# Reordering the first batch of a fused attention and MLP kernel

## The chip, the cores and the metric

The kernel runs on one NeuronCore of a Trainium2 chip. The metric is the device time in microseconds (us) of one execution; lower is better. The engines are TensorE (PE, with its weight loads PEld), VectorE (DVE), ScalarE (ACT), GpSimd (POOL) and the queue engine SyncE (SP), which issues most DMAs. Each engine works through its own list of instructions in order; a wait for another engine holds up everything behind it in that list.

## The reference

Eight batches of block-recurrent cross attention are followed by an MLP with a softplus-erf activation. All arithmetic is float32; the two MLP weights arrive as float64 and are turned into float32 in the kernel.

```python
# x: (B=8, H=8, S=512, D=64), state: (8, 8, Ns=32, 64)
scores = x @ state^T / sqrt(D);  a  = softmax over the 32 states
xread  = a @ state                                   # 512 rows per batch and head
scores2 = state @ x^T / sqrt(D); a2 = softmax over the 512 tokens
sread  = a2 @ x                                      # 32 rows per batch and head
tokens = concat([xread, sread], axis=2)              # (8, 8, 544, 64) -> (4352, 512)

h  = tokens @ w_in                                   # w_in (512, 2048)
sp = softplus(h)
out = (h * erf(sp)) @ w_out                          # w_out (2048, 512)
```

The kernel doesn't form xread. For each batch it multiplies the state with w_in first (the "M sets", four per batch, one for each group of 512 hidden features), and the hidden layer of the 512 tokens is then `a @ M`.

## The kernel before

Batch 0 is written out by hand, since the weights have to be fetched and converted at the same time. Sixteen pieces of 1 MB come in the order w_in 0, w_in 1, w_out 0, w_out 1, w_in 2, and so on; in the code they are `"i", 0`, `"o", 0` and so on. A piece passes through one of three raw buffers. It is converted by two ScalarE and three VectorE instructions, and the third VectorE instruction of one piece calls `fetch()` for the next.

```python
def weight(dst, src, shape):
    raw = act.tile([...], U32, name="raw", bufs=3)
    fetched.append(nc.sync.dma_start(out=raw..., in_=src...))
    ...
    return [ACT: dst = hi * 2**-112,  ACT: lo = lo * 2**-29], \
        [DVE: d <<= 3,  DVE: d += lo,  DVE: d |= sign of hi]        # written short here

def on_act(kind, j, ks=range(2)):
    for k in ks: made[kind, j][0][k]()
def on_dve(kind, j, ks=range(3)):
    for k in ks:
        made[kind, j][1][k]()
        if k == 2: fetch()
```

The first batch's attention: x's chunks are turned on TensorE, the scores of all heads are made by 16 small matmuls, and VectorE and ScalarE do the softmax over the states. `between` are pieces of other work, called at fixed places.

```python
for c in range(NC):
    (nc.scalar, nc.sync)[c % 2].dma_start(out=x_t[0][:, c], in_=x[0, :, P * c:P * c + P]...)
    if c == 1:
        for e in range(2):
            nc.sync.dma_start(out=st[:, 0, D * e:D * e + D], in_=state[0]...)

def attention0(between):
    ...
    for c in range(NC):
        for i in range(NI):
            nc.tensor.transpose(out=xp[i][:, P * c:P * c + P], in_=xt[:, c, 2 * i:2 * i + 2, :], identity=ident)
        if c == 1:
            states(range(1))                      # turn and copy state 0
    for i in range(NI):
        (nc.scalar.copy, nc.vector.tensor_copy)[i % 2](xT[:, i, :], xp[i])
    s2 = scored(0, xT)
    between[0]()                                  # 20 warming matmuls; w_in 0 on ACT
    for e in range(2):
        nc.vector.transpose(out=both[:, e], in_=s2[e])
        nc.vector.reduce_max(out=m1, in_=a, axis=AX.X)
        nc.vector.tensor_tensor(a, a, over(m1), op=ALU.subtract)
        nc.scalar.activation(out=a, in_=a, func=ACTF.Exp, scale=scale)
        nc.scalar.copy(sc[:, e], s2[e])
    between[1]()                                  # w_in 1 on ACT, w_in 0 on DVE
    for e in range(2):
        normalise(...)                            # sum, add 1e-9, reciprocal, multiply
        nc.vector.transpose(out=aT[0][:, e], in_=both[:, e])
```

An M set takes 16 matmuls for its two PSUM banks and a copy of each bank. For each of the 16 feature tiles of batch 0, `first0` makes the hidden values of 512 tokens with two matmuls, `soft` and `keep_h` read them from PSUM with ScalarE and VectorE, `erf` and `times` finish the activation, and `project` multiplies with w_out.

```python
def mixed_part(b, g, j, parts, copy):            # part j of M set g
    for i in range(NI):
        for e in range(2):
            nc.tensor.matmul(out=ps[e][q, :], lhsT=st[r, b, q], rhs=w_in[r, fs, i, :], ...)
    return nc.scalar.copy(mg[:, 0], ps[0]), copy(mg[:, 1], ps[1])

# the middle of batch 0, group 1 and the start of group 2 (cut from the whole)
done(project(g0[0], 0, acc, range(NC), range(2)))
on_dve("o", 1); times(Z, g0)
for j in 2, 3:
    convert("i", j)
done(project(g0[0], 0, acc, range(3), range(2, 4)))
on_act("o", 2)
mixed(0, 1, copy=nc.scalar.copy)                 # a whole M set
done(project(g0[0], 0, acc, range(3, 4), range(2, 4)))
...
for i in range(GF):
    first0(2, i, g2[0]); soft(i, g2); keep_h(i, g2); on_dve("o", 5, ...)
```

Up to this point the order of each engine's list is fixed to that of the code (`in_order`). From batch 1 on, `hidden7` and `project7` do 2x2 block products with seven instead of eight multiplications. They need differences of blocks: of M (`combine_m`), of the attention weights (`combine_a`) and, once for all batches, of w_out (`combine_w`):

```python
def combine_w():
    sub(T[1], B12, B11); sub(T[2], B22, T[1]); sub(T[4], B21, T[2])    # 128x2048 each
    def last():
        sub(B12, B22, B12); T[3] = B12
    return last

# after batch 0
in_order(begun)
next(turn)
combine_m(1, 1 - begins(1))
last = behind(at, combine_w)
for b in range(1, B + 1):
    ...  # hidden7 of one group runs while project7 of the one before is stepped
```

Of the kernel before, what the change touches and what calls it, by code (L numbers as in the profile page):

```python
# [16 lines left out]
def kernel(  # L17
# [90 lines left out]
    for c in range(NC):  # L108
        (nc.scalar, nc.sync)[c % 2].dma_start(
            out=x_t[0][:, c], in_=x[0, :, P * c:P * c + P].rearrange("h p d -> p h d"))  # L110
        if c == 1:
            for e in range(2):
                nc.sync.dma_start(out=st[:, 0, D * e:D * e + D],
                                  in_=state[0].rearrange("(i e) n d -> e i n d", e=2)[e])
# [76 lines left out]
    def scored(b, xT):  # L191


        s2 = [ps_at.tile([P, S], F32, name="at") for _ in range(2)]
        for i in range(NI):
            for e in range(2):
                r, q = slice(D * e, D * e + D), slice(Ns * i, Ns * i + Ns)
                on_pe = nc.tensor.matmul(out=s2[e][q, :], lhsT=st[r, b, q], rhs=xT[r, i, :],  # L198
                                         start=True, stop=True)
        marks.append(on_pe)  # L200
        return s2
# [10 lines left out]
    def normalise(a):  # L212
        z1 = small.tile([P, NC * NI], F32, name="z1")
        nc.vector.reduce_sum(out=z1, in_=a, axis=AX.X)
        nc.vector.tensor_scalar(z1, z1, 1e-9, None, op0=ALU.add)
        nc.vector.reciprocal(z1, z1)
        return nc.vector.tensor_tensor(a, a, over(z1), op=ALU.mult)  # L217
# [54 lines left out]
    def attention0(between):  # L272
# [7 lines left out]
        for c in range(NC):  # L280
            for i in range(NI):
                nc.tensor.transpose(out=xp[i][:, P * c:P * c + P],
                                    in_=xt[:, c, 2 * i:2 * i + 2, :], identity=ident)
            if c == 1:
                states(range(1))
        for i in range(NI):
            (nc.scalar.copy, nc.vector.tensor_copy)[i % 2](xT[:, i, :], xp[i])
        s2 = scored(0, xT)
# [3 lines left out]
        aT[0] = keep.tile([P, 2, S], F32, name="aT")  # L292
        for e in range(2):
            nc.vector.transpose(out=both[:, e], in_=s2[e])
            a = both[:, e].rearrange("p (k n) -> p k n", n=Ns)
            m1 = small.tile([P, NC * NI], F32, name="m1")
            nc.vector.reduce_max(out=m1, in_=a, axis=AX.X)
            nc.vector.tensor_tensor(a, a, over(m1), op=ALU.subtract)
            nc.scalar.activation(out=a, in_=a, func=ACTF.Exp, scale=scale)
            nc.scalar.copy(sc[:, e], s2[e])  # L300
        between[1]()
        for e in range(2):
            normalise(both[:, e].rearrange("p (k n) -> p k n", n=Ns))
            nc.vector.transpose(out=aT[0][:, e], in_=both[:, e])
# [22 lines left out]
    def attention(b, xT=None):  # L327
# [10 lines left out]
        aT[b] = keep.tile([P, 2, S], F32, name="aT")  # L338
        for e in range(2):
            nc.vector.transpose(out=both[:, e], in_=sc[:, e])  # L340
            a = both[:, e].rearrange("p (k n) -> p k n", n=Ns)
            m1 = small.tile([P, NC * NI], F32, name="m1")
            nc.vector.reduce_max(out=m1, in_=a, axis=AX.X)  # L343
            nc.vector.tensor_tensor(a, a, over(m1), op=ALU.subtract)  # L344
            nc.scalar.activation(out=a, in_=a, func=ACTF.Exp, scale=scale)
        z2 = weigh_tokens(sc, largest(sc), both[:, 2:4])
        for e in range(2):
            normalise(both[:, e].rearrange("p (k n) -> p k n", n=Ns))
            nc.vector.transpose(out=aT[b][:, e], in_=both[:, e])  # L349
# [18 lines left out]
    def mixed(b, g, parts=1, copy=nc.vector.tensor_copy):  # L368

        m_t[b, g] = mix.tile([P, 2, gw], F32, name="m")  # L370
        return [mixed_part(b, g, j, parts, copy) for j in range(parts)]

    def mixed_part(b, g, j, parts, copy):
# [9 lines left out]
        return nc.scalar.copy(mg[:, 0], ps[0]), copy(mg[:, 1], ps[1])  # L383
# [143 lines left out]
    def combine_w():  # L527
        T[1], T[2], T[4] = (act.tile([P, 2 * GF * P * 2], U32, name="raw", bufs=3).bitcast(F32)
                            .rearrange("p (g i e) -> p g i e", i=GF, e=E2) for _ in range(3))
        sub = lambda o, x, y: nc.vector.tensor_tensor(o, x, y, op=ALU.subtract)  # L530
        sub(T[1], B12, B11)
        sub(T[2], B22, T[1])
        sub(T[4], B21, T[2])

        def last():
            sub(B12, B22, B12)
            T[3] = B12
        return last
# [59 lines left out]
    def begins(b):  # L598
        return 1 - b % 2
# [31 lines left out]
    def prepare(b, g, copy):  # L631
        for j in range(2):
            mixed(b, 2 * g + j, copy=copy)
        combine_m(b, g)

# [59 lines left out]
    def after_scores():  # L695
        warm(20)
        on_act("i", 0)

    def before_sums():
        on_act("i", 1)  # L700
        on_dve("i", 0)

    rest = attention0((after_scores, before_sums))
    m_t[0, 0] = mix.tile([P, 2, gw], F32, name="m")
    mixed_part(0, 0, 0, 2, nc.scalar.copy)
    warm(6)
    on_act("o", 0)
    g0 = group()
    first0(0, 0, g0[0])
    first0(0, 1, g0[0])  # L710
    soft(0, g0)
    on_dve("i", 1)
    on_act("o", 1, [0])
    keep_h(0, g0)
    soft(1, g0)
    mixed_part(0, 0, 1, 2, nc.scalar.copy)
    on_dve("o", 0, [0])
    keep_h(1, g0)
    on_dve("o", 0, [1, 2])
    first0(0, 2, g0[0])  # L720
    first0(0, 3, g0[0])
    erf(A, g0)
    times(A, g0)
    on_act("o", 1, [1])
    for i in 2, 3:
        soft(i, g0)
        keep_h(i, g0)
    erf(Z, g0)
    acc = tiles(NC)
    done(project(g0[0], 0, acc, range(NC), range(2)))  # L730
    on_dve("o", 1)
    times(Z, g0)
    for j in 2, 3:
        convert("i", j)
    done(project(g0[0], 0, acc, range(3), range(2, 4)))
    on_act("o", 2)
    mixed(0, 1, copy=nc.scalar.copy)
    done(project(g0[0], 0, acc, range(3, 4), range(2, 4)))
    on_dve("o", 2)
    on_act("o", 3)  # L740
    g1 = group()
    first0(1, 0, g1[0])
    first0(1, 1, g1[0])
    soft(0, g1)
    keep_h(0, g1)
    on_dve("o", 3, [0, 1])
    soft(1, g1)
    keep_h(1, g1)
    on_dve("o", 3, [2])
    first0(1, 2, g1[0])  # L750
    first0(1, 3, g1[0])
    erf(A, g1)
    times(A, g1)
    on_act("i", 4)
    for i in 2, 3:
        soft(i, g1)
        keep_h(i, g1)
# [3 lines left out]
    convert("i", 5)  # L761
    done(project(g1[0], 1, acc, range(NC), range(2)))
    done(project(g1[0], 1, acc, range(2), range(2, 4)))
    on_act("o", 4)
    mixed(0, 2, copy=nc.scalar.copy)
    done(project(g1[0], 1, acc, range(2, 3), range(2, 4)))
    on_dve("o", 4)
    load_st()
    on_act("o", 5)
    g2 = group()  # L770
    for i in range(GF):
        first0(2, i, g2[0])
        soft(i, g2)
        keep_h(i, g2)
        on_dve("o", 5, range(i, i + 1) if i < 3 else ())
    done(project(g1[0], 1, acc, range(3, 4), range(2, 4)))
    load_xq(1)
# [5 lines left out]

    finish_(g2)
    next(rest)
    done(project(g2[0], 2, acc, range(1)))
    convert("i", 6)
    for bs in range(1, 5), range(5, B):
        states(bs)
    convert("i", 7)  # L790
    done(project(g2[0], 2, acc, range(1, 3)))
    next(rest)
    on_act("o", 6)
    mixed(0, 3, copy=nc.scalar.copy)
    next(rest)
    on_dve("o", 6)
    xT, _ = turn_x(1)
    g3 = group()
    for i in 0, 1:
        first0(3, i, g3[0])  # L800
        soft(i, g3)
        keep_h(i, g3)
    next(rest)
    load_x(1)
    for i in 2, 3:
        first0(3, i, g3[0])
        if i == 2:
            on_act("o", 7)
            on_dve("o", 7, [0, 1])
        soft(i, g3)  # L810
        keep_h(i, g3)
    on_dve("o", 7, [2])
    done(project(g2[0], 2, acc, range(3, 4)))
    finish_(g3)

    turn = attention(1, xT)
    next(turn)
    next(turn)
    seconds = project(g3[0], 3, acc)
# [4 lines left out]

    some(4)
    for k in range(2):
        for j in range(2):
            mixed(1, 2 * (begins(1) ^ k) + j, copy=nc.scalar.copy)
            some(2 if not k else 1)
        if k == 0:  # L830
            combine_m(1, begins(1))
            at = [combine_a(1)]
    in_order(begun)
    next(turn)
    combine_m(1, 1 - begins(1))
    last = behind(at, combine_w)
# [5 lines left out]
    for b in range(1, B + 1):  # L842
# [4 lines left out]
        for g, (first, second) in enumerate(groups):  # L847
# [3 lines left out]
            if b + 1 < B:  # L851

                if g == 0:
                    turn = attention(b + 1)
                    side[6 - (b == 1)] = lambda: behind(marks, next, turn)
                elif g == 1:
                    side[0] = lambda: (next(turn), next(turn))
# [14 lines left out]
            gT_ = first(lambda: next(steps))  # L872
            done(steps)
            if last is not None:
                last()
                last = None
# [34 lines left out]
```

## Time and profile before

The time is 759.62 us, the median of 3 runs (758.96 to 761.93); the profiled execution spans 758.7 us.

| what | value |
|---|---|
| matmul of one projection step (128x512) | about 0.86 us of stream, two records |
| seven-product matmuls, 128x256, 480 of one kind | 118.1 us busy, mean 380 ns |
| conversion of one piece on ACT | 2 instructions, 1.15 us each |
| conversion of one piece on DVE | 0.69, 1.23 and 1.23 us |
| difference of w_out blocks, 128x2048 | 2.29 us |
| load of one weight piece, issue to landing | 4.7 to 5.6 us (median by kind) |
| HBM read and written | 33.03 MB and 8.91 MB |

In the profile each row of a timeline has the start, the length, the engine, the line of the kernel, the operation, what it writes and reads, and in brackets how long its engine sat idle before it and what ended that. L672 is `first0`, L679 `keep_h`, L676 `soft`, L685 `times`, L508 `project`, L381 the M sets, L150 the last conversion step, L452 the matmuls of `hidden7`, L460 its additions, L530 the differences of w_out and L558 `project7`. A wait table has the waiting instruction, who released it, the total in us, how often, and the longest. A TensorE float32 matmul can show as two records.

### The profile page before, as it was taken

The page shows a single profiled execution, that of the slowest core. Times are in us where ns is not written, and L with a number is a line of the kernel's source. Part 1 is how long each engine was busy: PE and PEld are TensorE (multiplying, and loading weights), DVE is VectorE, ACT ScalarE, POOL GpSimd, SP SyncE. Part 2 cuts the span into 40 slices and gives each one's busy share as a digit, 9 for nine tenths or more (in the row PEclk, how much of TensorE's full clock was granted, in tenths as well). Part 3 has the DMA queues.
Part 4 walks back from the last instruction along what each step waited for, and adds up shares of the span by engine and source line. Part 5 has one row for each costly group of instructions (what it writes and reads, how often), then busy time and mean ns, then how long its engine had stood idle before and what let it go on. Part 6 is the DMA issues. An engine that isn't in the chain of part 4 may idle for free.

```text
span 758.7 us, 11976 instructions
## 1 busy us (share of the span) xinstructions
PE 733.8 (97%) x4934; PEld 585.1 (77%) x4934; DVE 524.7 (69%) x775; ACT 390.4 (51%) x488; POOL 0.7 (0%) x6
## 2 busy tenths in 40 slices
PE   7899899799999999999999999999999999999997
PEld 5333343687888888888888888888888889999996
DVE  3887888786759476876677665866696765585423
ACT  3878784485444634644355545554365444443330
POOL 0000000000000000000000000000000000000000
PEclk9999999899999999999999999999999999999999
DMA  7565752261024100610052003310021000000000
GB/s 225 167 222 183 183 133 40 55 130 32 22 61 82 27 29 2 140 29 29 1 108 57 16 17 72 79 20 29 20 65 29 29 1 29 1 29 1 21 8 28
DMA packets 139165, 46.38 MB, mean 61 GB/s; under 512 B 126696, under 2 KB 130536, under 8 KB 139112
## 3 DMA queue, kind: packets, MB, share of 16 engines
q1 hardware_dynamic: 136744, 44.78, 23.6%
q10 hardware_dynamic: 2368, 0.85, 0.5%
q8 instruction: 38, 0.62, 0.3%
q14 instruction: 15, 0.12, 0.1%
HBM read 33.03 MB, written 8.91 MB: 55 GB/s over the span
## 4 chain that ended last, share of the span: by engine, by line
PE 82%; DVE 6%; ACT 2%; issue 0%; DVEq 0%; ACTq 0%
PE o L558 47%; PE h L452 26%; PE at L381 3%; PE o L508 2%; PE h L672 1%; PE at L257 1%; DVE raw L530 1%; PE at L198 1%; DVE hs L460 0%; DVE aT L349 0%; DVE xT L344 0%; DVE xT L217 0%; DVE xT L340 0%; DVE m L343 0%; DVE m L222 0%
## 5 line engine op out<-in xcount | busy, mean ns | idle before, releaser
L459 ACT ACTIVATE s<-hs 128x512 f32<-128x512 f32 x120 | 75.6, 630 | 105.9 <-DVE hs L460 105.5
L558 PE MATMUL o<-w_out,s 128*128 128x256 f32 x480 | 118.1, 380 | 0.0
L558 PE MATMUL o<-raw,hs 128*128 128x256 f32 x480 | 117.0, 385 | 0.1
L503 DVE TENSOR_TENSOR s<-s,hs 128x2048 f32<-128x2048 f32 x30 | 68.8, 2292 | 68.4 <-ACT s L502 68.4
L558 PE MATMUL o<-w_out,hs 128*128 128x256 f32 x480 | 114.1, 380 | 0.0
L558 PEld LDWEIGHTS o<-raw,hs 128*128 128x128 f32 x480 | 88.8, 190 | 32.3 <-issue 19.3
L558 PEld LDWEIGHTS o<-w_out,hs 128*128 128x128 f32 x480 | 90.6, 190 | 16.4 <-issue 4.2
L452 PEld LDWEIGHTS h<-aT,m 128*128 128x128 f32 x672 | 85.7, 194 | 11.2 <-DVE hs L460 4.6
L460 DVE TENSOR_TENSOR hs<-hs,h 128x512 f32<-128x512 f32 x90 | 61.5, 684 | 46.6 <-PE h L452 46.6
L452 PE MATMUL h<-aT,m 128*128 128x128 f32 x672 | 87.8, 279 | 4.7 <-DVE hs L460 3.8
L558 PEld LDWEIGHTS o<-w_out,s 128*128 128x128 f32 x480 | 84.6, 191 | 8.1
L460 DVE TENSOR_TENSOR hs<-s,h 128x512 f32<-128x512 f32 x60 | 41.1, 685 | 42.0 <-PE h L452 41.4
L508 PE MATMUL o<-w_out,s 128*128 128x512 f32 x128 | 59.1, 602 | 2.5 <-DVE s L685 2.5
L452 PE MATMUL h<-sy,sx 128*128 128x128 f32 x448 | 59.7, 275 | 1.2 <-ACT hs L468 0.7
L452 PEld LDWEIGHTS h<-sy,sx 128*128 128x128 f32 x448 | 56.7, 192 | 3.7 <-ACT hs L468 1.5
L558 PE MATMUL o<-raw,s 128*128 128x256 f32 x240 | 57.6, 379 | 0.0
L502 ACT ACTIVATE s<-s 128x2048 f32<-128x2048 f32 x30 | 57.3, 1911 | 0.3
L468 ACT COPY hs<-h 128x512 f32<-128x512 f32 x30 | 17.6, 587 | 77.0 <-PE h L452 77.0
L463 ACT COPY s<-h 128x512 f32<-128x512 f32 x30 | 17.5, 582 | 76.9 <-PE h L452 76.9
L508 PEld LDWEIGHTS o<-w_out,s 128*128 128x128 f32 x128 | 23.0, 190 | 35.5 <-issue 26.7
L558 PEld LDWEIGHTS o<-raw,s 128*128 128x128 f32 x240 | 43.5, 190 | 4.7
L459 ACT ACT_TABLE_LOAD x32 | 41.1, 1283 | 0.6
(120 smaller groups left out, 904.9 us busy)
## 6 DMA issues: line engine op xcount, KB each, us to landing
raw<-in_moe_w_in_dram SPq DMA_DIRECT2D x8, 1024.0 KB, 5.6
raw<-in_moe_w_out_dram SPq DMA_DIRECT2D x8, 1024.0 KB, 4.7
xq<-in_x_dram SPq DMA_DIRECT2D x112, 64.0 KB, 2.1
x<-in_x_dram SPq DMA_DIRECT2D x56, 128.0 KB, 2.7
out_dram<-ot SPq DMA_DIRECT2D x18, 256.0 KB, 2.1
sc<-xT SPq DMA_DIRECT2D x112, 32.0 KB, 1.9
out_dram<-ot SPq DMA_DIRECT2D x28, 128.0 KB, 1.7
x<-in_x_dram ACTq DMA_DIRECT2D x2, 256.0 KB, 5.2
```

The costliest lines, as they stand in the source:

```text
L198: on_pe = nc.tensor.matmul(out=s2[e][q, :], lhsT=st[r, b, q], rhs=xT[r, i, :], start=True, stop=True)
L257: nc.tensor.matmul(out=sr[q, e, :], lhsT=a2T[:, e, c, q], rhs=xt[:, c, 2 * i + e, :], start=(c == 0), stop=(c == NC - 1))
L381: nc.tensor.matmul(out=ps[e][q, :], lhsT=st[r, b, q], rhs=w_in[r, fs, i, :], start=True, stop=True)
L452: last = nc.tensor.matmul(out=bank[:, q], lhsT=lhsT, rhs=rhs, start=(first and i == 0 and k == 0), stop=(i == GF - 1 and k == len(ops) - 1 ...
L459: nc.scalar.activation(out=s[:, k], in_=hs[:, k], func=ACTF.Softplus)
L460: add = lambda o, x, y: nc.vector.tensor_tensor(o, x, y, op=ALU.add)
L463: nc.scalar.copy(m1, p)
L468: nc.scalar.copy(c11, p)
L502: return (nc.scalar.activation(out=s, in_=s, func=ACTF.Erf), nc.vector.tensor_tensor(s, s, hs, op=ALU.mult))
L503: nc.vector.tensor_tensor(s, s, hs, op=ALU.mult))
L508: nc.tensor.matmul(out=acc[r], lhsT=gT[:, i, P * r:P * r + P], rhs=w_out[:, GF * g + i, :], start=(g == 0 and i == 0), stop=(g == NG - 1 a ...
L558: nc.tensor.matmul(out=acc[bank][:, E2 * c:E2 * c + E2], lhsT=lhs[:, i, :], rhs=rhs[:, g, i, :], start=(first and i == 0 and c == 0), stop ...
```

## The change

It reorders the first batch and the passage into the second, and leaves the sum of the mathematics as it is. Its purposes: to have x complete sooner; to let VectorE and ScalarE alternate in the softmax; to make an M set available by halves, each after one weight piece; to keep VectorE's copies from waiting for ScalarE; and to take the long differences of w_out out of the way of the second batch's additions.

```diff
     for c in range(NC):
         (nc.scalar, nc.sync)[c % 2].dma_start(... x chunk c ...)
-        if c == 1:
-            for e in range(2):
-                nc.sync.dma_start(out=st[:, 0, D * e:D * e + D], ...)
+    for e in range(2):
+        nc.sync.dma_start(out=st[:, 0, D * e:D * e + D], ...)
...
-        for i in range(NI):                      # scored
+        for i in reversed(range(NI)):
...
+    def states_weights(b, sc, both):             # also used by the later batches
+        for e in range(2):
+            nc.vector.transpose(out=both[:, e], in_=sc[e])
+        for e in range(2):
+            nc.vector.reduce_max(out=m1[:, e], in_=a[:, e], axis=AX.X)
+        for e in range(2):
+            nc.vector.tensor_tensor(a[:, e], a[:, e], over(m1[:, e]), op=ALU.subtract)
+            nc.scalar.activation(out=a[:, e], in_=a[:, e], func=ACTF.Exp, scale=scale)
...
+    def normalise(a, between=lambda: None):      # both halves share add and reciprocal
+        for e in range(2):
+            nc.vector.reduce_sum(out=z1[:, e], in_=a[:, e], axis=AX.X)
+        between()
         nc.vector.tensor_scalar(z1, z1, 1e-9, None, op0=ALU.add)
         nc.vector.reciprocal(z1, z1)
+        for e in range(2):
+            nc.vector.tensor_tensor(a[:, e], a[:, e], over(z1[:, e]), op=ALU.mult)
...
-        for c in range(NC):                      # attention0
+        for c in 1, 0, 2, 3:
             ... transposes of chunk c ...
-            if c == 1:
-                states(range(1))
         ... copies of xT ...
+        states(range(1))
...
     def after_scores():
-        warm(20)
+        warm(28)
         on_act("i", 0)
     def before_sums():
         on_act("i", 1)
-        on_dve("i", 0)
+        on_dve("i", 0, [0, 1])
+    def amid_sums():
+        on_dve("i", 0, [2])
+        on_act("o", 0, [0])
+        m_t[0, 0] = mix.tile([P, 2, gw], F32, name="m")
+        mixed_part(0, 0, 0, 2, nc.scalar.copy, nc.scalar.copy)
-    mixed_part(0, 0, 0, 2, nc.scalar.copy)
-    warm(6)
-    on_act("o", 0)
```

In the groups of batch 0 the same calls are set in a new order, with M sets 1 to 3 in halves. `evict(i, gT, True)` calls `keep_h` before `soft`. The core of it:

```diff
-    for j in 2, 3:
-        convert("i", j)
-    done(project(g0[0], 0, acc, range(3), range(2, 4)))
-    on_act("o", 2)
-    mixed(0, 1, copy=nc.scalar.copy)
-    done(project(g0[0], 0, acc, range(3, 4), range(2, 4)))
+    convert("i", 2)
+    on_act("i", 3)
+    on_act("o", 2, [0])
+    some0(0, g0, range(2), range(2, 4))
+    mixed_part(0, 1, 0, 2, nc.scalar.copy, nc.scalar.copy)
+    some0(0, g0, range(2, 3), range(2, 3))
+    on_dve("i", 3)
+    load_st()                                    # states 1 to 7, was in group 2
+    on_act("o", 2, [1])
+    first0(1, 0, g1[0])
+    on_dve("o", 2, [0])
+    evict(0, g1, True)
+    mixed_part(0, 1, 1, 2, nc.scalar.copy, nc.scalar.copy)
...
+    for bs in range(1, 5), range(5, B):
+        states(bs)                               # was after group 2
...
+    load_xq(1)                                   # was after group 2's hidden values
...
-    turn = attention(1, xT)                      # after group 3's activation
-    next(turn)
-    next(turn)
-    seconds = project(g3[0], 3, acc)
-    some(4)
-    ... four M sets of batch 1, with 2, 2, 1, 1 steps after them ...
+    turn = attention(1, xT)                      # ahead of group 3, taken in four steps
+    ...
+    some(2)
+    ... four M sets of batch 1, with 3, 3 and 4 steps between and after ...
```

The differences of w_out and of the second M pair, in the passage to batch 1:

```diff
-    def combine_w():
-        sub(T[1], B12, B11); sub(T[2], B22, T[1]); sub(T[4], B21, T[2])
-        def last(): sub(B12, B22, B12); T[3] = B12
+    def combine_w(g, last=False):                # half g: 128x1024 each
+        if last:
+            sub(T[3], B22, B12)
+        else:
+            sub(T[1], B12, B11); sub(T[2], B22, T[1]); sub(T[4], B21, T[2])
...
-    combine_m(1, 1 - begins(1))
-    last = behind(at, combine_w)
...
             gT_ = first(lambda: next(steps))
+            if b == 1 and g == 0:
+                combine_m(1, 1 - begins(1))
+                behind(marks, combine_w, begins(1))
             done(steps)
+            if b == 1 and g == 0:
+                combine_w(begins(1), True)
+            if b == 1 and g == 1:
+                behind(marks, combine_w, 1 - begins(1))
+                behind(marks, combine_w, 1 - begins(1), True)
```

`marks` are the last matmul and the last addition of the `hidden7` just written; `behind` keeps the differences after them. In the later batches `attention` is taken in five steps instead of three, with the same work but for the shared add and reciprocal, and the second batch's scores move two steps up (`side[6 - (b == 1)]` to `side[6 if b > 1 else 3]`).

## The prediction

> **What bounds the kernel now.** I read the shares of busy time first, then the 40 slices, then a table of stretches, TensorE's waits, and last the timeline where TensorE stood still.
>
> ```profile
> PE 733.8 (97%) x4934; PEld 585.1 (77%) x4934; DVE 524.7 (69%) x775; ACT 390.4 (51%) x488; POOL 0.7 (0%) x6
> ...
> PE   7899899799999999999999999999999999999997
> ```
>
> TensorE is the bound: 25 us of 758.7 are idle, nearly all in the first nine slices of 19 us, which is where the change works. The stretches (length, busy time of each engine, granted clock, DMA share, GB/s) say how much there is to win:
>
> ```profile
> 24.00:34.00 10.00, 8.31 (x35) 3.01 (x33) 9.74 (x12) 8.47 (x11) 0.00 (x0) 1.00 0.39 135
> 34.00:83.00 49.00, 45.56 (x128) 17.89 (x128) 37.23 (x41) 37.78 (x41) 0.00 (x0) 1.00 0.64 203
> 83.00:127.50 44.50, 42.03 (x247) 17.02 (x248) 37.49 (x57) 34.01 (x53) 0.00 (x0) 1.00 0.54 119
> 127.50:154.00 26.50, 20.93 (x184) 16.36 (x183) 22.48 (x25) 11.80 (x16) 0.00 (x0) 0.87 0.31 70
> 154.00:200.00 46.00, 44.44 (x288) 38.62 (x288) 36.27 (x62) 28.14 (x36) 0.00 (x0) 1.00 0.31 64
> 200.00:700.00 500.00, 499.86 (x3609) 428.18 (x3608) 349.19 (x535) 242.56 (x302) 0.00 (x0) 1.00 0.17 38
> ```
>
> Length less PE busy gives the idle time: 1.7, 3.4, 2.5, 5.6 and 1.6 us, then 0.1 us in 500. From 127.5 to 154 the mean clock is 0.87, which costs another 0.13 x 26.5 = 3.4 us. So between 24 and 200 us there are 14.8 + 3.4 = 18.2 us that a perfect order could win; before 24 us everything hangs on the softmax. Who ends TensorE's waits between 24 and 154 us:
>
> ```profile
> PE h L452 <- DVE hs L460: 4.8, 2, 3.8
> PE o L508 <- DVE s L685: 2.5, 4, 1.6
> PE h L672 <- DVE hs L679: 1.6, 3, 0.6
> PE at L381 <- DVE w_in L150: 1.5, 2, 1.1
> ```
>
> The first line is one event, and VectorE's timeline shows its cause:
>
> ```profile
> 129.66 2.29 DVE L530 TENSOR_TENSOR raw<-w_out 128x2048 f32<-128x2048 f32 x1
> ...
> 132.47 2.29 DVE L530 TENSOR_TENSOR raw<-w_out,raw 128x2048 f32<-128x2048 f32 x1
> ...
> 136.47 2.29 DVE L530 TENSOR_TENSOR raw<-w_out,raw 128x2048 f32<-128x2048 f32 x1
> 138.67 0.68 DVE L460 TENSOR_TENSOR hs<-s,h 128x512 f32<-128x512 f32 x1
> 139.27 2.29 DVE L530 TENSOR_TENSOR w_out<-w_out 128x2048 f32<-128x2048 f32 x1
> ```
>
> The four differences of w_out for the seven-product scheme sit in one block of VectorE. The addition that frees a PSUM bank (L460) stands behind them until 138.67, so TensorE waits 3.8 us at 139.41, 1.0 us more at 142.21, and then runs at half clock.
>
> **What the skill says.** The Trainium skill, "TensorE: Matmul & The Clock Gate", Part 1: The HAM clock gate, says that after an idle window of about 3.4 us the array's clock is halved until it has been busy about as long. The trace agrees: the granted clock is 0.50 from 140 to 146 us, after the gap of 3.8 us; it is also 0.50 from 21 to 23 us after a gap of only 2.8 us. The same page's "Architectural detail" has VectorE and ScalarE as strict first-in first-out queues; the L460 line behind the block is that. "ScalarE: Activation LUTs", What ACT_TABLE_LOAD costs, gives 1283 ns for a load and some 1380 ns of drain; the trace shows 32 loads of 1283 ns and no drain on top (a load at 54.88, the erf at 56.17). "DMA: Bandwidth & Descriptors", Issuing engines are not separate DMA queues, says that several issuers save only issue time; here one issue takes 0.46 to 0.74 us.
>
> **The change part by part.**
>
> *Loads and scores.* Before, the two loads of state 0 were issued ahead of x's chunk 3 (1.25 to 2.59 us), so chunk 3 was issued at 2.63. Now it goes out at about 1.25, the state after it, and the state's transpose stands after x's. Before, chunks 2 and 3 were turned from 8.10 to 10.02, behind the state's transpose, which waited 0.6 us for its load. I estimate their end at 9.0. The bytes are the same, so I don't expect more. The score matmuls ran from 10.05 to 12.88 (2.83 us), with VectorE's second copy of xT arriving at 10.9; the same 16 matmuls take 1.09 us later (110.25). With all operands there at 10.0, I put their end at 11.3: 1.6 us earlier.
>
> *Softmax halves alternated.* The six VectorE operations take 4.15 us (13.02 to 17.17) in either order; only ScalarE's exponential is better hidden. Then before: conversion of the first w_in piece (0.69, 1.23, 1.23, net 3.2), and two chains of sum, add, reciprocal, multiply, transpose at 2.6 us each, ending 25.58; 12.6 us in all. After: 4.15 + 3.15 + two sums 1.25 + one add and reciprocal 0.45 + two multiplies 1.25 + two transposes 1.3 = 11.55 us, from 11.3 to 22.85. The second aT is 2.7 us earlier. Against that, 28 warming matmuls at 0.25 us (20 took 5.01) end at 18.3, and the six that followed the first M set are gone: two gaps near 1.5 and 1.5 us with 0.7 us of work between, about the activity at which the clock fell before. I take off 0.7 us. **Net 2.0 us.**
>
> *M sets in halves, both copies on ScalarE, and the new order to 127 us.* A half needs one converted w_in piece instead of two: this aims at the 1.1 us at 47.78 (L381 on L150). VectorE copies come before ScalarE's softplus, so they no longer wait for it (VectorE idles 11.9 us ahead of them in the trace), which aims at the three L672 waits (1.6 us). Projections cut finer and set between other work aim at the four L508 waits (2.5 us). Idle from 24 to 127.5 is 7.6 us. Costs: a half takes 0.67 us against 1.09 for a whole, so 2 x 0.67 - 1.09 = 0.25 us each, 0.75 for three sets; one more table load on ScalarE (exponentials between softplus calls), 1.3 us, off TensorE's path. VectorE and ScalarE are busy 37 of 49 us from 34 to 83, so I expect new waits of about 3 us. 7.6 - 0.75 - 3 = **about 4 us.** As a second way I laid the three queues out row by row in program order with these durations (conversion 2.1 us on ScalarE and 3.1 on VectorE, copy 0.6, softplus 0.5, table 1.28, hidden matmul pair 1.8, projection 0.9), each step starting when its engine and its inputs are free: w_in's second piece ready at 25.9, first product and projection at 31.2 (before 34.2), second M set's first half at 42.0 (47.8), last hidden pair of group 2 done at 73.5 (81.2), group 1's projections done at 78.9 (82.8), and the seven-product stage begun at 120.3 (127.5) with 12 of 16 last projections done instead of 10. That is 9.0 us by then, start included, against 6.0 of my sum; it has no time between an event and the engine it frees, so I take it as the bright end.
>
> *States' loads and reads earlier.* Their DMAs are issued on the same queue as the weights: eight of about 0.6 us (5 us) and sixteen (10.5 us by the row of 16 issues at 126.57). The weights then lie two pieces ahead, so I count nothing.
>
> *Block differences in two parts.* 8.8 us of VectorE become two halves of 4 x 1.15 = 4.6 us, each held behind the seven-product stage's last addition. The idle 5.6 us and the half clock 3.4 us of 127.5 to 154 are 9.0 us. What stays: only 4 projection steps (0.86 us each) are left as filler instead of 6, while additions, softplus, table, erf (1.9) and multiply (2.3) take some 7 us before the first product can use them; the next group's products can fill most of it, as they did at 145.8 to 153.7. And the second 4.6 us fall into a stretch where VectorE was already full (10.0 of 10 us from 150 to 160) with batch 2's softmax. I leave 2.5 us: **about 6.5 us.**
>
> *From 200 us on.* One add and one reciprocal less per batch on VectorE, scores in reversed order: TensorE is 100% busy, so nothing.
>
> Sum: 2.0 + 4.0 + 6.5 = 12.5 us, 759.6 to 747.1; with a little of the bright end, **746.8 us**.
>
> **The rivals.**
> - *The wait moves to VectorE later.* The second part of the differences delays additions in 145 to 175 us, and a new gap, perhaps again with half clock, appears there. For: that stretch's full VectorE. Against: the differences are needed only at the third product of the following stage, and VectorE has 0.3 of its time free from 200 us on. It gives back 4 to 6 us: 751 to 753.
> - *The front of the kernel is worse.* Fewer warming matmuls around the first M set bring half clock into the first softplus matmuls, four of 1.7 us: 2 to 3 us, 749 to 750.
> - *ScalarE becomes the bound to 127 us*, with all copies of the M sets and of the conversions on it, in strict order. For: 9.9 of 10 us from 30 to 40. Against: over 34 to 83 it has 11 us free. The middle then brings 0 to 1: 750.
> - *All fits.* 16 to 17 us: 743.
>
> **Range and chances.** The rivals are not exclusive, and one half of each is likely; the ceiling is 18.2 + 2.7 = 21 us. 741.5 to 752 should hold it 8 times in 10. The line of 2% is 744.4 us, 15.2 us of gain: above my sum, below the layout. Faster by over 2%: 0.32; within: 0.65; slower: 0.03.
>
> **What would show it.** Right: no block of three 2.29 us differences, clock 1.00 through the start of the seven-product stage, first softplus matmul near 22 us, stage start near 120 to 122, idle of 24 to 127.5 at 3 to 4 us. Wrong: first softplus matmul still near 24 us or run at clock 0.5; more than 3 us of waits on L460's successor in 140 to 180; or a PE busy sum from 200 on that differs by over 2 us, which I have not counted at all.

## The result and the profile after

The changed kernel takes 750.2 us (median of 4 runs, 749.22 to 751.17) against 760.09 us for the kernel before in the same comparison: ratio 0.987, 95% interval 0.984 to 0.989. I had predicted 746.8 us with a range of 741.5 to 752. The gain is 9.9 us where my sum had 12.5. The two profiled executions span 758.7 and 749.4 us, 9.3 us apart.

The same stretches as before, from the changed kernel's table of stretches (length, then busy time of PE, PEld, DVE, ACT, POOL, then granted clock, DMA share, GB/s):

```profile
24.00:34.00 10.00, 9.12 (x36) 3.50 (x35) 9.84 (x13) 8.07 (x11) 0.00 (x0) 1.00 0.61 190
34.00:83.00 49.00, 48.19 (x174) 20.23 (x173) 39.15 (x47) 44.29 (x57) 0.00 (x0) 1.00 0.74 218
83.00:127.50 44.50, 43.55 (x287) 19.11 (x287) 38.72 (x58) 30.55 (x47) 0.00 (x0) 1.00 0.46 106
127.50:154.00 26.50, 23.51 (x202) 18.96 (x201) 22.16 (x33) 16.56 (x24) 0.00 (x0) 0.94 0.53 122
154.00:200.00 46.00, 44.17 (x301) 36.45 (x301) 37.21 (x53) 23.26 (x28) 0.00 (x0) 1.00 0.11 24
200.00:700.00 500.00, 499.07 (x3616) 430.62 (x3615) 344.69 (x519) 241.26 (x301) 0.00 (x0) 1.00 0.17 38
```

Length less PE busy: 0.9, 0.8, 0.9, 3.0, 1.8 and 0.9 us, where it was 1.7, 3.4, 2.5, 5.6, 1.6 and 0.1; the clock of the fourth stretch costs 0.06 x 26.5 = 1.6 us instead of 3.4. From 24 to 200 us that is 9.1 us lost instead of 18.2. The first three stretches are nearly clean. What is left lies in the passage to batch 1, and it is another wait than before. TensorE's waits from 24 to 154 us, the longest first:

```profile
PE h L457 <- ACT s L468: 1.9, 1, 1.9
PE h L674 <- DVE aT L313: 1.6, 1, 1.6
PE h L674 <- ACT m L387: 1.1, 2, 0.5
PE at L197 <- DVE sn L279: 1.0, 1, 1.0
PE h L457 <- ACT hs L473: 0.7, 1, 0.7
```

The wait on VectorE's addition is down from 4.8 to 0.4 us, that on `times` from 2.5 to 0.2, and those on the copies of the first batch (1.6) and on the converted w_in (1.5) are gone. In their place TensorE waits for ScalarE to copy a bank (L468). ScalarE's timeline shows why it is late:

```profile
133.64 1.91 ACT L507 ACTIVATE s<-s 128x2048 f32<-128x2048 f32 x1
135.46 0.57 ACT L522 COPY ot<-o 128x512 f32<-128x512 f32 x1
135.92 0.59 ACT L468 COPY s<-h 128x512 f32<-128x512 f32 x1
```

The copy stands behind the first group's erf and one copy of a finished output tile. TensorE's own timeline of that place:

```profile
130.77 1.02 PE L513 MATMUL o<-w_out,s 128*128 128x512 f32 x2
131.63 1.05 PE L457 MATMUL h<-aT,m 128*128 128x128 f32 x8
132.53 1.06 PE L457 MATMUL h<-sy,sx 128*128 128x128 f32 x8
133.51 1.10 PE L273 MATMUL at<-x,sc 128*32 128x64 f32 x64
136.56 1.16 PE L457 MATMUL h<-aT,m 128*128 128x128 f32 x8 [1.95 <-ACT s L468]
138.40 1.76 PE L457 MATMUL h<-sy,sx 128*128 128x128 f32 x8 [0.68 <-ACT hs L473]
139.95 3.43 PE L565 MATMUL o<-w_out,s 128*128 128x256 f32 x10
```

The last projection step is done at 131.6; then come two products of the next group and the state's read, and TensorE has nothing more that it may start. The eight matmuls at 138.40 take 1.76 us where the same eight took 1.06 at 132.53: the clock is 0.50 from 139 to 142.

Whether the copy or the want of work sets this gap, which part of the change gave what, and why the loads brought nothing, were the open questions.

### The profile page after: what moved, and what is told of

It is laid out like the page before. It is cut to its first block, busy times and chain, and to the rows that moved or that the text cites. A ratio compares the mean times of both kernels' runs of the same rounds, so it can differ in the third digit from the quotient of the medians.

```text
span 749.4 us, 12076 instructions
## 1 busy us (share of the span) xinstructions
PE 730.8 (98%) x4986; PEld 584.4 (78%) x4986; DVE 522.2 (70%) x763; ACT 388.6 (52%) x493; POOL 0.7 (0%) x6
## 4 chain that ended last, share of the span: by engine, by line
PE 78%; DVE 8%; ACT 1%; issue 0%; DVEq 0%
PE o L565 44%; PE h L457 24%; PE at L385 4%; PE o L513 3%; DVE hs L465 2%; PE at L197 1%; DVE aT L353 1%; PE h L674 1%; DVE xT L233 1%; DVE z L228 1%; DVE m L238 1%; PE at L273 1%; DVE xT L221 1%; ACT s L507 1%; DVE hs L562 0%; DVE hs L561 0%
## 5 line engine op out<-in xcount | busy, mean ns | idle before, releaser
L457 PE MATMUL h<-aT,m 128*128 128x128 f32 x672 | 86.3, 276 | 3.1 <-ACT s L468 3.1
L468 ACT COPY s<-h 128x512 f32<-128x512 f32 x30 | 17.5, 585 | 97.1 <-PE h L457 97.1
L464 ACT ACT_TABLE_LOAD x31 | 39.8, 1283 | 0.5
```

The lines of the kernel that those rows point to most:

```text
L457: last = nc.tensor.matmul(out=bank[:, q], lhsT=lhsT, rhs=rhs, start=(first and i == 0 and k == 0), stop=(i == GF - 1 and k == len(ops) - 1 ...
L464: nc.scalar.activation(out=s[:, k], in_=hs[:, k], func=ACTF.Softplus)
L468: nc.scalar.copy(m1, p)
```

## The experiments

All ratios are to the kernel before, run on the same chip beside them. The medians of the kernel before lay between 760.1 and 761.8 us, so ratios are compared and not times.

### What the divided differences are worth

The kernel before with this part alone, and the changed kernel without it:

```diff
 # e1: the kernel before
-    combine_m(1, 1 - begins(1))
-    last = behind(at, combine_w)
+    (combine_w(g, last) by halves and combine_m after the first stage, as in the change)
 # e2: the changed kernel: the same lines the other way round
```

> The kernel before with one part of the change alone: w_out's differences in two halves behind the seven-product stages, and M's second pair combined after the first stage. If the gain of the passage (idle plus half clock there fell from 10.5 to 6.4 us) stands by itself: 4 us off, about 755.5 to 756. Rival, that the passage only gains because the first batch leaves it in another state: 1 us or less, 758.5 or more.

Measured: 756.24 us, ratio 0.9928 (0.9910 to 0.9946), so 5.5 us off. In the trace the passage has another picture than before, in e1's table of stretches:

```profile
127.50:154.00 26.50, 23.33 (x209) 18.43 (x208) 24.00 (x34) 15.50 (x20) 0.00 (x0) 1.00 0.40 93
154.00:200.00 46.00, 44.74 (x300) 37.85 (x299) 37.25 (x61) 26.23 (x33) 0.00 (x0) 1.00 0.25 51
```

Idle 3.2 + 1.3 us and the clock at 1.00 throughout, against 5.6 + 1.6 and 3.4 us of clock before: the part does what it is for. What is left is the same gap as in the changed kernel: after the fourth projection step TensorE waits 1.6 us for a bank copy on ScalarE and 0.7 us for the next. So the reordered first batch did not make this gap. That the clock did not fall holds for the execution traced (mean 1.000); the other three show 0.992 to 0.998.

> The changed kernel with the differences of w_out in one block of four, and M's second pair combined ahead of the first stage, as before. If first batch and passage add up: 750.2 + 4 = 754.2, with the 3.8 us wait on the addition and some 6 us of half clock back. Rival, the same time is lost either way for want of ready work: 751 to 752.

Measured: 753.72 us, ratio 0.9895 (0.9880 to 0.9909). It lies between the two expectations. TensorE waits 4.2 us for VectorE's additions again:

```profile
PE h L457 <- DVE hs L465: 4.2, 2, 2.5
```

and nothing else in 120 to 200 us. So the part is worth 5.5 us by itself. On top of the rest it is 0.9895 - 0.987 = 0.0025 of 760, some 2 us, and there the intervals overlap; the traced spans, 752.0 and 749.4, say 2.6 us. The two parts do not add: alone they bring 5.5 and 8.0 us, together 9.5 to 10.

### The gap at 135 us

```diff
 # e3: more work kept back          # e4: the copy moved
-    some(4)                        -        nc.scalar.copy(m1, p)
+    some(1)                        +        (nc.vector.tensor_copy if (b, g, h) == (1, 1 - begins(1), 0)
     in_order(begun)                +         else nc.scalar.copy)(m1, p)
```

> The changed kernel with 7 instead of 4 of the last 16 projection steps kept for the seven-product stage (same work, later). Theory, TensorE runs out of ready work there because the first activation takes 7 us after the last addition: the waits of 1.95 and 0.68 us near 135 and the half clock of 139 to 142 vanish, 3 to 4 us off, about 747. Rival, the cause is ScalarE's order (the copy that frees the bank stands behind the erf): the wait stays, 750.

> The changed kernel with the first bank copy of the second seven-product stage on VectorE instead of ScalarE, so that it no longer stands behind the erf. If ScalarE's order is the cause: the 1.95 us wait and with it the half clock go, 3 to 4 us off, about 747. If want of ready work is the cause: TensorE does its next eight matmuls earlier and then waits for the product of the activation instead, at most 1 us off, 749.5 to 750.

Measured: e3 750.05 us, ratio 0.9856 (0.9834 to 0.9879), profile span 747.5; e4 750.41 us, ratio 0.9852 (0.9838 to 0.9867), span 748.9. Neither reaches 3 to 4 us. In e3 the gap is closed: from 119.4 to 154 us TensorE is busy 33.3 of 34.6 us at full clock. Two other waits took over, in e3's waits from 119 to 200 us:

```profile
PE h L457 <- ACT hs L473: 1.5, 1, 1.5
PE h L457 <- DVE sy L429: 1.0, 1, 1.0
PE h L457 <- DVE hs L465: 0.3, 1, 0.3
```

The stage starts 2.5 us earlier, and VectorE has not made the differences of the attention weights (L429) by then. In e4 the wait of 1.95 us became one of 0.9 us on ScalarE's next copy, the clock stayed at 1.00, and project7 began at 140.6, no earlier than the 139.95 of the changed kernel. This is not a clean test of the copy: the free order of this stretch changed too. VectorE turned the next batch's x (L330) ahead of the multiplication, which began at 137.2 instead of 136.6, and TensorE did the next scores before project7 instead of after it. A like stage further on, which starts at 180.88 in the changed kernel, starts at 180.3 in e4 and at 178.9 in e3. So more ready work brings 1.9 us in the trace and the earlier copy 0.6: want of ready work is the larger part. That e3 is faster than the changed kernel in time is not shown by the two intervals.

```diff
 # e8: the first half of the differences waits for the multiplication that ends the first group
-                behind(marks, combine_w, begins(1))
+                behind(finished, combine_w, begins(1))
```

> The changed kernel with the first half of w_out's differences held until after the multiplication that ends the first seven-product group, instead of only after its last addition. In the trace after, that multiplication starts at 136.6, 1.1 us after the erf it needs, behind the differences. If it sets when project7 may start: 1 us off, ratio 0.9855. If TensorE's wait is for its bank copy on ScalarE alone: no change, 0.987.

Measured: 751.47 us, ratio 0.9871 (0.9851 to 0.9891), beside the unchanged kernel's 0.9875 below. The multiplication starts at 135.4 instead of 136.6, but project7 begins at 141.3, with the clock halved there for longer (0.90 on average from 120 to 154 us, against 0.95). An earlier multiplication by itself brings nothing. But here too the free order changed: the next scores and part of the next M set came ahead of project7, so it is not shown that VectorE's order has no share in the gap.

### The loads, the score order and the warming matmuls

```diff
 # e5: the changed kernel, with the part below as before
-    (chunk 3 ahead of the state's load; chunks turned 1, 0, 2, 3, the state last; scores in reversed order)
+    (state's load ahead of chunk 3; chunks 0 to 3, the state after chunk 1; scores in order)
 # e6: the changed kernel
-        warm(28)
+        warm(20)
```

> The changed kernel with the loads of x and of state 0, the order in which x's chunks and the state are turned, and the order of the score matmuls as before. My prediction's step says that this part brings 1.6 us: 751.8. By the trace after, the scores end at 12.9 us as before, since the last chunk lands no earlier: 750.2, within 0.5.

> The changed kernel with 20 instead of 28 warming matmuls after the scores. The scores and the softmax are the same, so TensorE then idles from about 18.5 us instead of 20.8. If that halves the clock as it did before the change: clock 0.5 for some 3 us around the first hidden matmuls, 1 to 1.5 us slower, 751.5. If the softmax chain hides it: 750.2.

Measured: e5 750.88 us, ratio 0.9860 (0.9839 to 0.9882); e6 752.44 us, ratio 0.9883 (0.9860 to 0.9907). In time, e5 shows no gain from this part. Its timeline says more; first the changed kernel, then e5:

```profile
7.96 0.90 PE L298 MATMUL o<-ident,x 128*128 128x128 f32 x3 [1.14 <-DMA x<-in_x_dram]
...
8.87 0.85 PE L298 MATMUL o<-ident,x 128*128 128x128 f32 x3
...
10.98 1.96 PE L197 MATMUL at<-xT,st 64*32 64x512 f32 x16 [0.83 <-DVE xT L301]
...
21.22 0.79 PE L385 MATMUL at<-w_in,st 64*32 64x256 f32 x16 [0.41 <-DVE z L230]
23.65 3.67 PE L674 MATMUL h<-aT,m 128*128 128x512 f32 x8 [1.64 <-DVE aT L313]
```

```profile
8.93 0.85 PE L299 MATMUL o<-ident,x 128*128 128x128 f32 x3
...
10.03 1.97 PE L198 MATMUL at<-xT,st 64*32 64x512 f32 x16
...
20.24 0.79 PE L387 MATMUL at<-w_in,st 64*32 64x256 f32 x16 [1.79 <-DVE z L231]
22.66 6.24 PE L676 MATMUL h<-aT,m 128*128 128x512 f32 x8 [1.64 <-DVE aT L315]
```

The last chunk of x is turned at the same time in both (8.87 and 8.93), though its load was issued 1.35 us earlier in the changed kernel. The loads tell why. From issue to landing, first chunk 2 (on ScalarE's queue, issued at 1.25 in both) and then chunk 3 (issued at 1.26 and 2.64), in the changed kernel and in e5:

```profile
x<-in_x_dram ACTq DMA_DIRECT2D x1, 256.0 KB, 6.7
x<-in_x_dram SPq DMA_DIRECT2D x1, 256.0 KB, 5.8
```

```profile
x<-in_x_dram ACTq DMA_DIRECT2D x1, 256.0 KB, 5.9
x<-in_x_dram SPq DMA_DIRECT2D x1, 256.0 KB, 6.1
```

So chunk 3 did land earlier, at about 7.0 instead of 8.7, but chunk 2 landed later, at 7.9 instead of 7.15. TensorE turns chunk 2 first, waits for it until 7.96, and the early chunk 3 stands behind it.

With the new order the scores then start 1 us later: the reversed order asks first for the part of xT that VectorE copies last, and the state's copy on ScalarE (10.29 to 10.57) comes after two others. The old loads make the softmax weights 1.0 us earlier in this trace. But the 28 warming matmuls then end before the M set is ready, and the first eight hidden matmul records take 6.24 us instead of 3.67. The clock of e5 is 1.00 up to 21 us and then 0.50:

```profile
21.00:27.00 6.00, 4.36 (x8) 1.85 (x6) 5.74 (x8) 2.48 (x5) 0.00 (x0) 0.50 0.53 175
```

e6 shows the same fall with the new loads: clock 0.50 at 24 to 26 us, the eight records in 5.19 us, the first projection at 33.8 instead of 32.6. The warming matmuls are worth about 1.2 us in the trace. In time the interval of e6 overlaps with that of the changed kernel, so this is shown by the trace alone.

### Softplus before copy, and whole M sets

```diff
 # e7
-        for f in (keep_h, soft) if late else (soft, keep_h):
+        for f in (soft, keep_h):
 # e10: on_dve of the second piece moved ahead of the set, for sets 1 to 3
-    mixed_part(0, 1, 0, 2, ...)  ...  mixed_part(0, 1, 1, 2, ...)
+    mixed(0, 1, nc.scalar.copy, nc.scalar.copy)
```

> The changed kernel with ScalarE's softplus ahead of VectorE's copy everywhere in the first batch. If the order matters because the second reader of a bank waits for the first: VectorE's conversions slip by the 3 to 4 us that ScalarE now waits, TensorE's idle time from 24 to 120 grows from 2.6 to 4 or 5 us, 752. Rival, it only swaps which engine waits: 750.2.

Measured: 751.21 us, ratio 0.9864 (0.9840 to 0.9888): the rival. VectorE waits 9.8 us for softplus from 24 to 120 us, where in the changed kernel ScalarE waits 3.9 us for the copies; TensorE's idle time there is 3.0 us instead of 2.7.

> The changed kernel with M sets 1 to 3 of batch 0 whole again, each placed after the conversion of both its w_in pieces. Halves cost 3 x 0.25 us of TensorE; if they win by being ready after one piece, whole sets bring back waits for the conversion of about 1 us each: 752. Rival, the conversions are early enough in the new order: 749.5.

Measured: 764.11 us, ratio 1.0036 (1.0026 to 1.0046): 13 us lost, more than the whole change brings. e10's waits from 24 to 120 us:

```profile
PE at L385 <- DVE w_in L149: 9.1, 3, 3.7
```

Three waits of 2.9, 2.4 and 3.7 us, one for each whole set, and after two of them the set itself takes 1.96 us instead of 1.09, at half clock. In this order the rest of TensorE's work stands behind the set. An order with other filler ahead of a whole set, as the kernel before had, was not tried.

### Putting it together

```diff
 # e12: e5 and              # e13: e12 and
-        warm(28)           -    some(4)
+        warm(36)           +    some(1)
```

> The changed kernel unaltered, as the yardstick of these four on one chip. Both theories: a ratio to the kernel before of 0.987.

Measured: 752.37 us, ratio 0.9875 (0.9858 to 0.9892).

> The changed kernel with x's loads, turning order and score order as before (which gave softmax weights 1.0 us earlier, but then the clock fell to 0.5 from 21 to 27.5 us) and 36 instead of 28 warming matmuls, to bridge that gap. If the old loads are the better ones and only the clock hid it: first projection at 31.5 instead of 32.6, clock 1.00 from 20 on, 1 us off, ratio 0.9855. If the clock falls anyway: 0.987 to 0.988.

Measured: 749.94 us, ratio 0.9852 (0.9830 to 0.9874). The first projection starts at 31.84 instead of 32.55, 0.7 us earlier where 1.1 was expected, and the clock is 1.00 all through the front, though it falls again near 139 us (0.95 on average from 120 to 154). The trace confirms the direction; the interval overlaps with that of the changed kernel.

> The last one, and besides it 7 instead of 4 projection steps kept for the first seven-product stage. If both gains are real and add: 1 us and 1 to 2 us, 747.5 where the changed kernel has 750.2, ratio 0.983 to 0.984. If the second is given back as before (the stage then waits 1 us for VectorE at its start): 0.9855.

Measured: 747.36 us (747.10 to 747.61), ratio 0.9812 (0.9796 to 0.9828). This one is clear of the changed kernel, by 0.0063 of 761.8 or 4.8 us, and beats both kernels. Its passage, from e13's table of stretches:

```profile
120.00:154.00 34.00, 32.74 (x251) 25.84 (x252) 30.91 (x50) 20.63 (x29) 0.00 (x0) 1.00 0.48 104
```

Idle 1.3 us at full clock, against 3.0 us at 0.95 for the changed kernel in the same stretch. The traced executions differ by less (745.8 against 749.5, 3.7 us), which is the sum of what e3 and e12 gain alone in theirs (747.5 and 747.6 against 749.4, 1.9 and 1.8 us). The rest is in the executions that were not traced: three of the changed kernel's four span 750.4 to 750.8 us at a mean clock of 0.995, where the traced one had 0.998, while e13's four span 745.3 to 745.8 at 0.999 to 1.000.

## Why the prediction held, and which term was off

**Loads and scores, 1.6 us: wrong.** The scores ended at 12.9 us in both kernels, not at 11.3. The first step that failed is that chunk 3, issued earlier, would complete x by 9.0. It landed 1.7 us earlier, but chunk 2, which is turned first, landed 0.8 us later, and both were turned by 9.93. Both traces move 226 to 227 GB/s from 2 to 7 us; that the two loads share this rate was argued and not tried, and neither was turning chunk 3 ahead of chunk 2. The second step is the scores. I took all their operands as ready at 10.0, and overlooked that the reversed order and the later state put them at 11.0. And I took the 16 matmuls at the 1.09 us that they need later: each lasts 1.06 us in the traces of both kernels, and 0.59 at the end of the same row in e5. With the old order the scores ended 0.5 to 0.9 us sooner than in the changed kernel in e5, e12 and e13; in the trace of the kernel before, where all 16 were slow, they did not.

**Softmax, 12.6 to 11.55 us: right.** From the first transpose to the second aT it took 11.0 us (13.12 to 24.10). The first projection started at 32.55 instead of 34.15: 1.6 us for the front, where the net term was 2.0. That the net came out near is luck. I had taken off 0.7 us for a fall of the clock after two gaps of 1.5 us. The gaps were 0.4 and 1.6 us and the clock held, because the scores ended 1.6 us later than I had them and the 28 warming matmuls took 7.94 instead of 7.0 us. With the scores 0.9 us earlier (e5) the same 28 were too few, and the clock fell; e6 shows that eight fewer would have cost 1.2 us.

**Middle, about 4 us: right.** The seven-product stage began at 121.95 instead of 127.5, 5.55 us; less the front, 3.95 us. The idle time of 24 to 120 us is 2.7 us, near my 3 us of new waits. Of the parts, the halves of the M sets are shown to matter (e10) and copying before softplus is not (e7); the finer projections were not taken back by themselves. My second way, the layout, had 9.0 us at this point. It started at 120.3, and it credited 1.7 us for 12 instead of 10 projections done; the trace of the kernel before had 12 done as well. So the 6 steps of filler that I gave the kernel before were a wrong reading too: both kernels had 4 left. The "32 loads" of tables are those of one line; the whole trace has 84, all of 1283 ns.

**Passage, about 6.5 us: right in mechanism, too large.** By the start of a like stage later (190.61 before, 180.88 after) the lead is 9.73 us, so the passage gave 4.2. The term that was mis-sized is "I leave 2.5 us" of the stretch from 127.5 to 154: idle time and half clock there are 3.0 + 1.6 = 4.6 us. The row that I named as filler (the next group's products) needs its PSUM banks emptied, by ScalarE and by VectorE, and those were behind the erf and the multiplication; so only two products ran ahead, a gap opened, and the clock fell again. e3 shows that more filler closes it. e1, in the kernel before, has the same gap and the same 4 steps, but no fall of the clock in its trace, and the part brought 5.5 us.

**From 200 us on, nothing: nearly.** The idle time rose from 0.1 to 0.9 us, and the lead fell from 9.73 to 9.3.

Of the rivals, VectorE's later load did not come true: the wait moved to ScalarE's copies. The front at half clock is real (e5, e6), and was avoided by the 28 warming matmuls. ScalarE as the bound did not come true either: it became busier, 44.3 of 49 us from 34 to 83, yet TensorE's idle time there fell from 3.4 to 0.8 us. Of my signs, the stage start (121.95), the block of differences and the idle time spoke for the prediction; the first softplus matmul at 23.65, near 24, and the clock in the passage spoke against it, and they point at the two terms that were off. The sum with the measured terms: 1.6 + 3.95 + 4.2 - 0.4 = 9.3 us.

## What to carry to other kernels

When a long block is taken out of an engine's order, ask what the engine that waited has to do until the next result is there: here 4 steps of filler were too few, and 7 closed the gap. Two gains that each change the moment at which an engine runs dry need not add: the differences and the first batch did not, e3 and e12 nearly did. A reordering that makes a chain shorter must be tried together with the filler that it leaves short: the earlier softmax was worth nothing with 28 warming matmuls and showed in the trace with 36. When a load is issued earlier, look at the landing of its neighbours as well: here chunk 3 gained 1.7 us and chunk 2, which was needed first, lost 0.8.

## What was unexpected of the hardware

The clock fell to 0.50 in e5 though no single gap was longer than 1.8 us: TensorE idled 1.8 us, worked 0.8 and idled 1.6. In the changed kernel gaps of 0.4 and 1.6 us about the same M set left it at 1.00. No length of a single gap separates the cases: at this place a gap of 2.8 us halved the clock in the kernel before, and one of 3.1 us in e1, whose front is the same code, did not.

20 warming matmuls took 5.0 us in the kernel before and 6.4 in e6, and a score matmul 1.06 us in the changed kernel and 0.59 at the end of e5's row, all in stretches for which the traces give a granted clock of 1.00. So in the first 20 us the same matmuls can take up to 1.8 times as long with no sign of it in that column; why is not shown.
